# A two-layer decode step on one core: wo in longer runs, o permuted by matmuls, a later return of stashed V, rstd moved behind the projections

## The chip, the core and the metric

One core of a Trainium2 chip runs the whole program. The metric is the device time of one execution in microseconds (us): 214.02 us, the median of three runs (213.67 to 215.77). The engines: TensorE (PE; its weight loads are shown apart as PEld), VectorE (DVE), ScalarE (ACT), GpSimd (POOL), and SyncE (SP), which here only issues DMAs.

## What is computed

Four sequences decode one token each (B = 4, D = 512) through four residual steps: attention, GLU, attention, GLU. Both attentions use the same weights and the same K and V, and so do both GLUs.

```python
def attention(x, k_cache, v_cache, wq, wo):      # Hq=32, Hkv=8, Dh=128, Sk=8192
    W = 2048                                     # the last 2048 keys
    q = (x @ wq) as [B, Hq, 1, Dh]
    k, v = the last W keys of each of 8 heads, each used by 4 query heads
    p = softmax(q k^T * Dh**-0.5);  o = p v
    return o as [B, 1, Hq*Dh] @ wo

def glu(x, w_gate, w_up, w_down):                # F=1792
    return (sigmoid(x @ w_gate) * (x @ w_up)) @ w_down

x = x + attention(layernorm(x), ...);  x = x + glu(layernorm(x), ...)
x = x + attention(layernorm(x), ...);  x = x + glu(layernorm(x), ...)
```

All inputs are bf16. K and V of the window are 16.8 MB each, wq and wo 4.2 MB each, the three GLU weights 5.5 MB together.

## The kernel before

**Memory.** SBUF holds an arena of 50 slots of 128 partitions x 4 KB. K takes 32 of them for good, four a head (two tiles, each with two batches): it is loaded once, transposed in place by DVE in the first attention (`k_transpose`, L676 to L681), and used by both attentions. The other 18 slots make nine tiles of 1 MB. Through these pass, in the order of the list `loads`: wq (4 tiles), V of the first attention (16 tiles, two a head) with the four tiles of wo between them, the GLU weights (w_gate 2, w_up 2, w_down 2), wq again (4), V of the second attention in reversed order of heads, the GLU weights again. The four wo tiles stay from the first attention to the second, and so does one V tile of head 7 (KEEP_V). The other V tile of head 7 is stashed: at the end of the first attention four DVE transposes (`stash`, L490 to L496) put it into the PSUM banks 0 to 3, and four more (`load_stash`, L498 to L509) bring it back into a tile for the second attention.

**Who decides the order.** The program is written as a list of operations with tokens for what they read and write (`P.op`). When the last use of a tile is written down (`done`, L416), its slot goes to the next entry of `loads` at once (`fill`), so each transfer has one slot and waits for that slot's last readers; SP issues transfers strictly in that order. The other engines' orders come from a planner (`_schedule`, L86), a list scheduler that gives each operation a duration from the table `_TM`, and lets an engine pick, among the operations that could start within 60 ns of the earliest, the one written first. At run time each engine follows its fixed order and waits on semaphores.

**Layer norm** (L572 to L612), with x transposed (features on partitions, 4 column groups x 4 batches): DVE squares x and sums x and x squared over the groups (L577, L581); PE adds over partitions with a matrix of ones (L586); DVE makes mean, mean squared and variance (L589 to L595); ACT takes Ln and Exp (L598, L601) for the reciprocal deviation rstd; DVE subtracts the mean and multiplies by rstd into xn (L604, L609).

**q** (`q_proj`, L616 to L660), in two halves of four KV heads: 16 matmuls with xn as weights and wq as moving data (L628); a DVE transpose (L636) and a scaled copy to qh (L641); 16 small matmuls that repeat each head's q on four groups of 32 partitions (L652); an ACT copy to qrep (L659). For each head, `q_unit` then writes four blocks of 32 x 64 into the block-diagonal qbd, two by DVE (L670) and two by ACT (L673).

**One head of attention** (`softmax_unit`, `turn_p`, `pv_unit`, `wo_unit`): 16 score matmuls (L699) into a PSUM bank; DVE maximum (L707, L710, L713); ACT Exp with sums (L716); four permuting matmuls (L728), an ACT copy (L733) and a DVE transpose (L737) turn the probabilities; POOL splits the sums in three parts (L741 to L745), PE spreads them (L751), DVE takes the reciprocal (L758). Then 2 x 32 matmuls with V tiles as weights (L772), a DVE multiplication by the reciprocal (`oe`, L780) into onb, and 16 matmuls with wo as weights (L796) with 4 moving columns each (one query head's four batches), all heads and query heads summing into 16 columns of one PSUM bank. The scores of head ui+2 are written down ahead of the PV of head ui. After the last head DVE adds the sum to x (L834).

**GLU** (`glu`, L837): 16 matmuls each for w_gate and w_up (L854), a DVE transpose each (L861), the sigmoid as Exp, Ln(1+e), Exp(-) on ACT (L867, L870, L873), the product hT on DVE (L876), and the w_down matmuls, L931 in the first GLU and L907 in the last, after which two copies (L915, L917) and a DMA give the output.

The loads that the change or the prediction speak of:

```python
461  def load_wq(k):      # k == 1: tiles of two 4 KB runs a partition
476  def load_wo(hh):
477      load(("wo", hh), 4, "bw_1k", (2 * SLOT, wo_d[:, hh * 2 * REP:(hh + 1) * 2 * REP, :], False))
...
429  def load_k(h):       # 8 transfers of 256 KB a head
```

## Time and profile before

| | |
|---|---|
| median of three runs | 214.02 us (213.67 to 215.77) |
| profiled execution, by the device's clock | 214.02 us |
| its span, first to last instruction | 212.3 us |
| PE, DVE, ACT, POOL busy | 102.0, 90.2, 35.7, 14.7 us |
| read from HBM | 71.83 MB, 338 GB/s over the span |
| first attention | about 14 to 137 us |
| first GLU | about 137 to 149 us |
| second attention | about 152 to 200 us |
| last GLU and output | about 200 to 212 us |

The profile's page gives the busy share of each engine in 40 slices of 5.3 us, the chain of waits that ended last, and groups of instructions by line, with their idle time and what ended it. A table of stretches gives, for any stretch in us from the start: its length, the busy time of PE, PEld, DVE, ACT and POOL with the number of instructions, then the clock granted to TensorE, the DMA share and GB/s. A line of the timeline gives start, duration, engine, line, operation, what it writes and reads, shape and count, and in brackets the idle time before it with its releaser. A line of the waits gives who waited for whom, then total us, times and the longest. The trace also holds each DMA packet with size and duration.

### The profile page before, as it was taken

What the parts mean: (1) busy time and instruction counts of PE and PEld (TensorE: products, weight loads), DVE (VectorE), ACT (ScalarE), POOL (GpSimd) and SP (SyncE); (2) the same over time, 40 slices, a digit from 0 to 9 for tenths busy, and PEclk for the clock granted to TensorE, in tenths of its full rate; (3) what the DMA queues carried; (4) which work ended last, traced back from release to release, by engine and by line L of the source; (5) the groups of instructions that cost most, each with busy time, mean ns of one, the idle gap of its engine ahead of it and who ended that gap; (6) DMA issues with size and microseconds to landing.
All of it is one profiled execution on the core that took longest, in us unless ns stands there. A gap on an engine that the chain in (4) does not pass through costs nothing.

```text
span 212.3 us, 4510 instructions
## 1 busy us (share of the span) xinstructions
PE 102.0 (48%) x1944; PEld 56.3 (27%) x1944; DVE 90.2 (42%) x221; ACT 35.7 (17%) x100; POOL 14.7 (7%) x77
## 2 busy tenths in 40 slices
PE   0440304082450630540620455554368899996675
PEld 0000001041230220230220234412112455665622
DVE  5135778336448217328214430521367443541230
ACT  2002012131030300020110020020024443322020
POOL 4000001101010100010100010000001211111000
PEclk9999999999999999999999999999997555555555
DMA  6999999999999999999999999969999999999990
GB/s 225 420 346 279 279 281 288 411 292 306 350 319 348 350 318 338 258 266 396 283 276 308 348 423 403 377 218 389 360 417 414 412 425 421 418 415 409 406 372 27
DMA packets 16148, 72.13 MB, mean 340 GB/s; under 512 B 1912, under 2 KB 6016, under 8 KB 9472
## 3 DMA queue, kind: packets, MB, share of 16 engines
q1 hardware_dynamic: 16120, 71.84, 96.5%
q8 instruction: 15, 0.25, 0.5%
q14 instruction: 5, 0.04, 0.1%
q10 hardware_dynamic: 8, 0.00, 0.0%
HBM read 71.83 MB, written 0.00 MB: 338 GB/s over the span
## 4 chain that ended last, share of the span: by engine, by line
SPq 44%; DMA 33%; PE 17%; issue 3%; DVE 2%; ACT 1%
SPq L382 44%; DMA arena<-in_A_v_cache_dram 16%; DMA arena<-in_B_w_down_dram 12%; PE ps L699 5%; PE ps L772 5%; DMA arena<-in_A_wq_dram 5%; PE ps L728 2%; PE ps L907 1%; PE ps L796 1%; PE ps L628 1%; PE ps L931 0%; PE ps L854 0%; PE ps L751 0%; ACT prow L716 0%; DVE ebuf L636 0%
## 5 line engine op out<-in xcount | busy, mean ns | idle before, releaser
L772 PE MATMUL ps<-ebuf,arena 128*128 128x8 bf16 x1024 | 31.6, 168 | 52.2 <-DMA arena<-in_A_v_cache_dram 49.2
L680 DVE STREAM_TRANSPOSE arena<-arena 128x1024 f32<-128x1024 f32 x32 | 38.3, 1225 | 19.1 <-DMA arena<-in_A_k_cache_dram 19.1
L772 PEld LDWEIGHTS ps<-ebuf,arena 128*128 128x128 bf16 x1024 | 29.4, 104 | 59.1 <-DMA arena<-in_A_v_cache_dram 55.5
L699 PE MATMUL ps<-arena,qbd 128*16 128x512 bf16 x256 | 29.3, 602 | 25.7 <-DVE qbd L670 13.0
L707 DVE TENSOR_REDUCE nmax<-ps 128x1 f32<-128x512 f32 x16 | 11.0, 687 | 25.5 <-PE ps L699 25.5
L716 ACT ACTIVATE prow<-ps,nmax 128x512 bf16<-128x512 f32 x16 | 11.0, 687 | 48.6 <-DVE nmax L713 26.8
L699 PEld LDWEIGHTS ps<-arena,qbd 128*16 128x16 bf16 x256 | 6.4, 107 | 39.0 <-issue 24.9
L780 DVE TENSOR_TENSOR onb<-ps,rinv 128x16 bf16<-128x16 f32 x16 | 3.1, 192 | 31.9 <-PE ps L772 31.9
L673 ACT COPY qbd<-qrep 32x64 bf16<-32x64 bf16 x32 | 7.7, 241 | 52.7 <-PE ps L699 52.1
L741 POOL CAST s<-psm 128x1 bf16<-128x1 f32 x16 | 3.0, 186 | 172.3 <-ACT prow L716 172.3
L628 PE MATMUL ps<-arena,xn 128*4 128x512 bf16 x64 | 8.2, 610 | 8.0 <-DMA arena<-in_A_wq_dram 6.5
L733 ACT CAST prow<-ps 128x512 bf16<-128x512 f32 x16 | 9.4, 585 | 14.3 <-PE ps L728 14.2
L796 PE MATMUL ps<-onb,arena 128*128 128x4 bf16 x256 | 9.2, 167 | 2.4 <-DVE onb L780 2.4
L737 DVE STREAM_TRANSPOSE ebuf<-prow 128x256 f32<-128x256 f32 x16 | 6.8, 427 | 7.4 <-ACT prow L733 7.3
L728 PE MATMUL ps<-prow,perm 64*128 64x256 bf16 x64 | 9.3, 389 | 1.4 <-ACT prow L716 1.4
L796 PEld LDWEIGHTS ps<-onb,arena 128*128 128x128 bf16 x256 | 8.1, 104 | 3.3 <-DVE onb L780 2.0
L854 PE MATMUL ps<-arena,xn 128*4 128x448 bf16 x64 | 6.6, 564 | 4.7 <-DVE xn L609 3.1
L598 ACT ACTIVATE lnv<-lnv 128x4 f32<-128x4 f32 x4 | 0.8, 206 | 33.0 <-DVE lnv L595 33.0
L636 DVE STREAM_TRANSPOSE ebuf<-ps 128x512 f32<-128x512 f32 x4 | 2.9, 716 | 8.0 <-PE ps L628 7.8
L861 DVE STREAM_TRANSPOSE ebuf<-ps 128x448 f32<-128x448 f32 x4 | 2.6, 650 | 7.8 <-PE ps L854 6.9
L670 DVE COPY qbd<-qrep 32x64 bf16<-32x64 bf16 x32 | 5.3, 165 | 0.7 <-ACT qrep L659 0.2
L751 PEld LDWEIGHTS ps<-sel_b,s 128*128 128x128 bf16 x48 | 2.5, 106 | 8.2 <-issue 5.9
(61 smaller groups left out, 71.0 us busy)
## 6 DMA issues: line engine op xcount, KB each, us to landing
arena<-in_A_v_cache_dram SPq DMA_DIRECT2D x30, 1024.0 KB, 18.3
arena<-in_A_k_cache_dram SPq DMA_DIRECT2D x64, 256.0 KB, 16.8
arena<-in_A_wq_dram SPq DMA_DIRECT2D x8, 1024.0 KB, 9.6
arena<-in_A_wo_dram SPq DMA_DIRECT2D x4, 1024.0 KB, 25.2
arena<-in_B_w_gate_dram SPq DMA_DIRECT2D x4, 896.0 KB, 19.2
arena<-in_B_w_up_dram SPq DMA_DIRECT2D x4, 896.0 KB, 15.8
arena<-in_B_w_down_dram SPq DMA_DIRECT2D x2, 1024.0 KB, 12.4
arena<-in_B_w_down_dram SPq DMA_DIRECT2D x1, 768.0 KB, 6.8
```

The lines of the kernel that those rows point to most:

```text
L382: o = P.op("sync", name, 0.0, lambda e, dst=dst, src=src: e.dma_start(dst, src), r=r, w=w, dma_bytes=nbytes, dma_rate=tm[rate])
L628: last = pe.matmul(ps[32 * hh:32 * hh + NB, qb, :], xn[:, c * NB:(c + 1) * NB], tile_ap(s)[:, o + hh * 512:o + (hh + 1) * 512], start=(c = ...
L673: P.op("scalar", "qe%s_%d" % (tag, a), c_act(64), lambda s_, dst=dst, src=src: s_.copy(dst, src), r=rd, w=[("q", k2, a)])
L680: P.op("vector", "T%d_%d" % (h, t), c_dve(1024), lambda v, v32=v32: v.transpose(v32, v32), r=[("k", 4 * h + t // 2 * 2, x) for x in range( ...
L699: last = pe.matmul(ps[32 * gi:32 * gi + NR, bank, :], qbd[:, q0:q0 + NR], kt[:, cp // 2, cp % 2, b % 2], start=(cp == 0), stop=(cp == 3))
L707: lambda v: v.tensor_reduce(nmax[:, k2:k2 + 1], ps[:, bank, :], AXX, ALU.max),
L716: lambda a: a.activation(prow[:, :].rearrange("p (m x t) -> p m x t", x=16, t=2), ps[:, bank, :].rearrange("p (m t x) -> p m x t", x=16, t ...
L728: last = pe.matmul(ps[:, PBS[i], 0:256], perm[64 * i:64 * i + 64, jh * 128:(jh + 1) * 128], prow[64 * i:64 * i + 64, jh * 256:(jh + 1) * 2 ...
L733: lambda a: a.copy(prow[:, :].rearrange("p (y i t) -> p i y t", i=2, t=2), ps[:, PBS[0]:PBS[0] + 2, 0:256].rearrange("p i (y t) -> p i y t ...
L737: lambda v: v.transpose(ebuf[:, k2 * 256:(k2 + 1) * 256], prow[:, :].bitcast(F32)),
L772: last = pe.matmul(ps[:, ob, bp * 8:bp * 8 + 8], src[:, j * 128:(j + 1) * 128], ev[:, j % 2, j % 16 // 2, x0:x0 + 8], start=(j == 0), stop ...
L796: last = pe.matmul(ps[:, WB, c * NB:(c + 1) * NB], tile_ap(s)[:, o + r_ * D + c * 128:o + r_ * D + (c + 1) * 128], ov[:, r_ * NB:(r_ + 1) ...
```

## The change

- **wo.** A partition now holds four neighbouring rows of wo for a head, so that a run in HBM is 4 KB (REP = 4 rows of 1 KB) where it was 1 KB. Row 4p+m of a head's 512 lies on partition p, so o is to be brought into the same order: four matmuls with 0/1 matrices `permo` (`pm`) copy rows of o, a DVE multiplication with the mask `maskp` (`oq`) keeps the right query head in each 32-partition group, and the result onp has 16 columns for each m. The wo matmuls move 16 columns for 4, into 64 PSUM columns; after the last head a DVE reduction (`xr`) sums the four query heads, ahead of the addition to x.
- **Layer norm.** xn is x minus the mean, from PSUM directly; rstd is left out of it. The variance is computed afterwards from the centred squares (`ln_sq`, `ln_rd2`), summed by PE (`ln_var`) after the first group of projection matmuls, and ACT makes rstd with the score scale folded in. rstd multiplies q in the copy to qh, and the gate's argument (`gs`); in the GLU the up branch gets it through the denominator: 1 / ((1 + e) * std), by `ga` and a DVE reciprocal `gr`, which stand for two ACT functions.
- **q.** The 16 repeating matmuls, qrep and the four block copies a head go. For each head four matmuls (`qx`) with shifted identity weights of 32 rows write the block-diagonal form into one PSUM bank, and one ACT copy of 256 columns moves it to qbd.
- **Stash.** The stashed V tile comes back two loads later in the list, after two V loads in place of ahead of them; its four transposes, in another order of banks, also wait for the first qc of the second attention. The first scores of the second attention go to a bank of q (OBS[0], partly cleared by `zero_q`), not to bank 0, which holds the stash.
- Set-up: `eyew`, `maskp`, `permo` are made from the identity, which now lies in ebuf; eg lies in qbd; a constant 1/D replaces the ones in the norm's sums.

No line of `load_k` or `k_transpose` is in the diff.

```diff
-    wo_d = A_wo.rearrange("(q p) n -> p q n", p=128)
+    wo_d = A_wo.rearrange("(h p m) n -> p h (m n)", p=128, m=REP)
...
-            load(("wo", hh), 4, "bw_1k", (2 * SLOT, wo_d[:, hh * 2 * REP:(hh + 1) * 2 * REP, :], False))
+            load(("wo", hh), 4, "bw_4k", (2 * SLOT, wo_d[:, hh * 2:(hh + 1) * 2, :], False))
...
-                for n, b in enumerate(STASH):
+                for n, b in [(n, STASH[n]) for n in (1, 2, 3, 0)]:
...
-                    o.prio += 60
-                    if n == 3:
-                        after_q.append(o)
+                    o.deps.update(fresh)
...
+            P.op("tensor", "ln_sum" + tag, tm["pe_f32"],
+                 lambda t: t.matmul(mean, ones_d, lnr[:, 0:nb], start=True, stop=True),
...
+            P.op("vector", "ln_xn" + tag, ds,
+                 lambda v: v.tensor_tensor(bview(xn[:, :], b0, b1), bview(xT[:, 0:NX], b0, b1),
+                                           mean.unsqueeze(1).broadcast_to([128, NC, nb]), ALU.subtract),
...
+            def variance():
+                P.op("tensor", "ln_var" + tag, tm["pe_f32"],
+                     lambda t: t.matmul(msq, ones_d, lnr[:, NB:NB + nb], start=True, stop=True),
...
+                P.op("scalar", "ln_ln" + tag, c_act(NB),
+                     lambda a: a.activation(lnv[:, 0:nb], msq, ACTF.Ln, bias=EPS * sc, scale=sc),
+                P.op("scalar", "ln_rstd" + tag, c_act(NB),
+                     lambda a: a.activation(lnr[:, 0:nb], lnv[:, 0:nb], ACTF.Exp, scale=-0.5),
+                if not for_q:
+                    P.op("scalar", "ln_std" + tag, c_act(NB),
+                         lambda a: a.activation(lnd[:, 0:nb], lnv[:, 0:nb], ACTF.Exp, scale=0.5),
...
+                if variance is not None:
+                    variance()
...
+                     lambda v, qi=qi: v.tensor_tensor(
+                         qi.rearrange("p (b x) -> p b x", b=NB),
+                         ebuf[:, :].rearrange("p (x y) -> p y x", y=32)[:, 0:NB],
+                         lnr[:, 0:NB].unsqueeze(2).broadcast_to([128, NB, 4 * REP]), ALU.mult),
...
+                if k and n == 0:
+                    fresh.append(qc)
+                    P.op("vector", "zero_q", c_dve(160), lambda v, qb=qb: v.memset(ps[:, qb, 0:160], 0.0), r=[("qh", i)], w=[("pss", 2)], banks=(qb,))
+                    after = (qc,)
...
-            for a in range(4):
-                dst = qbd[32 * a:32 * a + 32, k2 * 256:(k2 + 1) * 256].rearrange(
...
+            def e_qx(pe):
+                for a in range(4):
+                    last = pe.matmul(dst[:, :, :, a * REP:(a + 1) * REP], eyew[32 * hh:32 * hh + 32, 96 - 32 * a:224 - 32 * a],
+                                     src, start=True, stop=True)
+            P.op("tensor", "qx" + tag, 250.0, e_qx, r=[("qh", h // 4), ("eyew",)], w=[("cb",)], banks=(CB,))
+            P.op("scalar", "qe" + tag, c_act(256),
+                 lambda a: a.copy(qbd[:, k2 * 256:(k2 + 1) * 256], ps[:, CB, 0:256]),
+                 r=[("cb",)], w=[("q", k2)], banks=(CB,))
...
+            bank, pt = (OBS[0], 2) if u == HKV else (SB[k2], k2)
...
+            def e_pm(pe):
+                for m in range(REP):
+                    last = pe.matmul(ps[:, ob, 144 + m * NR:144 + (m + 1) * NR], permo[:, m * 128:(m + 1) * 128], ov,
+                                     start=True, stop=True)
+            P.op("vector", "oq" + tag, tm["dve_fix"] + 60.0,
+                 lambda v: v.tensor_tensor(
...
-                        last = pe.matmul(ps[:, WB, c * NB:(c + 1) * NB],
+                        last = pe.matmul(ps[:, WB, c * NR:(c + 1) * NR],
-                                         ov[:, r_ * NB:(r_ + 1) * NB], start=(first and r_ == 0 and c == 0),
+                                         ov[:, r_ * NR:(r_ + 1) * NR], start=(first and r_ == 0 and c == 0),
...
+            P.op("vector", "xr%d" % L, c_dve(REP * NX),
...
+                if n == 0:
+                    variance()
...
+                    P.op("vector", "gs%d" % k, c_dve(NH),
+                    P.op("vector", "ga%d" % k, c_dve(NH),
+                    P.op("vector", "gr%d" % k, c_dve(NH) + 60.0,
...
-        load_stash(("V",) + keep[0] + (1,))
...
+                    n_v += 1
+                    if n_v == 2:
+                        load_stash(("V",) + keep[0] + (1,))
```

## The prediction, made before the changed kernel was run

> **What bounds the kernel now.** I read the page's slices first, then a table of stretches, the waits of the DMA queue, and the timeline of TensorE and of the last microseconds.
>
> ```profile
> span 212.3 us, 4510 instructions
> ...
> DMA  6999999999999999999999999969999999999990
> GB/s 225 420 346 279 279 281 288 411 292 306 350 319 348 350 318 338 258 266 396 283 276 308 348 423 403 377 218 389 360 417 414 412 425 421 418 415 409 406 372 27
> DMA packets 16148, 72.13 MB, mean 340 GB/s; under 512 B 1912, under 2 KB 6016, under 8 KB 9472
> ```
>
> The DMA engines are busy in every slice but three: the first, the last, and slice 26 (138 to 143 us). So the time is what the packets take, plus three holes. Busy is not fast: 270 to 350 GB/s in the first 118 us, 415 to 425 at the end.
>
> ```profile
> 20.00:30.00 10.00, 1.89 (x16) 0.44 (x16) 7.02 (x10) 0.48 (x2) 0.00 (x0) 1.00 1.01 278
> 35.00:37.00 2.00, 0.00 (x0) 0.00 (x0) 1.62 (x3) 0.00 (x0) 0.00 (x0) 1.00 1.10 321
> 63.00:66.00 3.00, 0.07 (x3) 0.00 (x0) 2.82 (x4) 0.52 (x1) 0.00 (x0) 1.00 1.09 266
> 92.00:96.00 4.00, 1.76 (x41) 1.16 (x37) 1.61 (x3) 0.58 (x1) 0.29 (x2) 1.00 1.09 271
> 116.00:118.00 2.00, 0.00 (x0) 0.00 (x0) 0.55 (x1) 0.00 (x0) 0.00 (x0) 1.00 1.04 344
> 139.00:142.00 3.00, 2.02 (x24) 0.51 (x24) 0.80 (x2) 0.27 (x2) 0.00 (x0) 1.00 0.38 125
> 151.00:155.00 4.00, 1.40 (x12) 0.21 (x16) 2.00 (x4) 0.39 (x2) 0.00 (x0) 1.00 1.03 422
> 160.00:195.00 35.00, 32.17 (x711) 19.00 (x700) 16.54 (x60) 14.06 (x37) 6.36 (x33) 0.54 1.01 417
> ```
>
> The last two columns are DMA share and GB/s. Row 1 is K alone. Rows 2 to 5 are the four wo tiles, 1 KB runs. Row 7 is wq of the second layer: 128 partitions, two 4 KB runs each. Row 6 is the hole. In row 8 PE is busy 32.2 of 35 us while the stream stays full.
>
> ```profile
> SPq L382 <- PE ps L854: 8.6, 4, 5.5
> ...
> 183.11 1.91 PE L699 MATMUL ps<-arena,qbd 128*16 128x512 bf16 x16
> 184.95 0.25 PE L751 MATMUL ps<-sel_b,s 128*128 128x16 bf16 x3
> 185.05 0.57 PE L796 MATMUL ps<-onb,arena 128*128 128x4 bf16 x16
> 185.47 1.85 PE L772 MATMUL ps<-ebuf,arena 128*128 128x8 bf16 x64
> 187.25 0.61 PE L728 MATMUL ps<-prow,perm 64*128 64x256 bf16 x4
> ...
> 206.74 0.22 DVE L876 TENSOR_TENSOR hT<-ebuf,eg 128x56 bf16<-128x56 f32 x1
> 207.40 2.25 PEld L907 LDWEIGHTS ps<-arena,hT 128*4 128x4 bf16 x28 [1.19 <-DMA arena<-in_B_w_down_dram]
> ```
>
> The hole: wd takes the slot of w_gate, so SP waits (up to 5.5 us) for the first GLU matmuls L854, behind PV, wo and the layer norm. One head of the second attention fills PE without a break, 4.7 us from one L728 to the next. At the end hT is done at 206.96 and PE starts at 207.40, when the last weights have landed: computation is only 0.4 us ahead of the stream. That decides what a shorter stream is worth. The sum is against this execution, 214.02 us by its clock (212.3 span and 1.7 around it), which is the median too.
>
> **The change, part by part.**
>
> *wo.* Same 4.19 MB, but 1,024 packets of 4 KB for 4,096 of 1 KB. In the trace's packet records a 1 KB packet takes 58 ns on average: 4,100 x 58 / 16 engines = 14.9 us, 281 GB/s. At row 7's 422 GB/s, the same tile shape, it is 9.9, a gain of 5.0. But wo was slow (266, 271) in two tiles and less so (321, 344) in two; if a cause beside it slows half of it by 266/344 still, the new time is 5.0 + 6.4 = 11.4, a gain of 3.5. If the cause were all in what lies beside it, the gain is 0. I take 4.2, near row 7 for its shape. The DMA page of the Trainium skill ("DMA: Bandwidth & Descriptors", Specifications) puts the smallest run for line rate at 512 B, by which 1 KB runs lose nothing. The trace has 281 against 422; by the rule the sum would be 4.2 us worse. No stall hides this term: the share is 1.0 in all these rows. Fewer packets can only let SP issue sooner.
>
> *The hole.* From the last PV's end (136.07) to L854 (139.66) is 3.6 us. Added: pm 0.30 (L751's three matmuls took 0.25), oq 0.27 (L641, same 128x64, 0.22 and a hop), xr 0.25 (reduction L581, 0.21). Gone: the square (0.21) and everything between the sum and xn, mean, two small DVE steps, Ln and Exp (1.04). Net -0.4; bounds -0.8 (pm costs nothing) and 0. The second norm (149 to 152) waits for wq landing: no gain. Variance, rstd and the gate's DVE steps lie beside the wait for w_up there (143.84): nothing; without that wait they cost what the end pays below. The first norm and the new masks lie before wq landing (7.0 to 13.4): nothing.
>
> So the stream would end 4.6 us sooner. The second attention starts as wq lands, so the computation moves by the same 4.6, and then:
>
> *PE per head.* qx: four matmuls of 64 columns. L699 moves 512 columns in 0.455 us (16 in 1.82, four at a time), so 0.057 each, 0.23 together; bounds 0.11 (PV's 28 ns each) and 0.40 (L652's whole group alone). pm: 4 at L751's 33 ns, 0.13; bounds 0.11, 0.25. wo with 16 columns for 4: L796 with 4 has 26 ns, L772 with 8 28 ns: nothing; at L751's 33 it is 0.11. Together 0.36 (0.22 to 0.76) in each of some six heads with PE full: +2.2 (1.3 to 4.6). Its cover in the first attention is the wait for V (L772 idle 52 us): nothing there. L728 works in a 64-row mode and its four took 0.54 in that chain, whatever the switch costs there. "TensorEngine Tiling (Array Packing)" of the skill (Tiling Modes, Key Properties) says that a change of tiling mode drains the engine, and qx brings a 32-row mode into each head; with two drains of 0.1 a head (an estimate from the 128 cycles of drain in "TensorE: Matmul & The Clock Gate", Part 2) the sum would be 1.2 worse.
>
> *Start of the second attention.* The four transposes of the stash (L504, 0.70 each) ran at 153 to 157, mostly while DVE waited. Now they need qc and the third wq tile, so they run from 158. DVE had 1.7 free before the first maximum at 160.08; 1.1 stay, ahead of that maximum, its exp and all P turns. Against it: half of the qe copies leave DVE (0.16 each), the 16 replication matmuls (0.30) leave PE twice, the first score matmuls no longer wait for them. But qc now waits for ln_var and two ACT steps, 0.35. Net +0.4 (-0.5 to +1.4). V goes out two loads sooner, but the stream is full there: nothing.
>
> *ACT and DVE per head.* Two copies of 0.24 on ACT become one of 0.37 (L659); two of 0.17 on DVE become oq, 0.22. ACT is under half busy: nothing, if the order holds (a rival).
>
> *End.* The chain PV to L854 is 0.4 shorter. After w_gate PE does ln_var (0.5, L586) ahead of w_up, and gs, ga, gr join DVE ahead of the second transpose: +0.5 (0 to 0.6), now with no landing to hide it.
>
> Computation: 2.2 + 0.4 - 0.4 + 0.5 = +2.7. The slack takes 0.4, so 2.3 is given back. Sum: -4.2 - 0.4 + 2.3 = -2.3, **211.7 us**: the stream no longer ends last, PE does.
>
> K's loads and transposes, named in the change's title, are not in the diff: the 64 issues of 256 KB and 278 GB/s stay.
>
> **Rivals.**
>
> *The additions hide.* If qx and pm fall into PE's gaps (1.7 us of "issue" at 194, 0.45 at 177), the stream's 4.6 all show: 214.0 - 4.6 = 209.4. For: those gaps. Against: the 4.7 us chain without a break.
>
> *wo does not get faster.* If something beside it sets its pace, as K's 8 KB packets crawl at 278, only the hole is won: 214.0 - 0.4 + 2.3 = 215.9. For: rows 3 and 4 against 2 and 5. Against: row 7, and all four wo rows lie below it.
>
> *PE waits in its own queue (the other side).* qx, the copy on ACT and the scores now form a chain. If the planned order puts the scores next behind qx, PE waits for ACT: up to an exp (0.88) and a copy (0.37), less 0.35 of overlap, 0.9 a head. Six heads: +5.4, 217.1. Behind it stand PV and wo, whose slots SP wants. It decides from 0.4 a head (2.3 / 6). For: one bank holds qx, and PE is in order. Against: qx of a head needs only the copy of the head before, so it can go a whole head early.
>
> **How the numbers follow.** Given back in part, 0.57 (own range 210.0 to 213.5); additions hidden 0.18; wo no faster 0.14; PE waits 0.11. About 1%, 2.1 us, is what a measurement of this kernel can tell from no change. Faster by that (under 211.9): 0.30 of the first and 0.18: 0.48. Slower (over 216.2): 0.11 and 0.02 of the third: 0.13. Within: 0.39. For 8 in 10 the range takes the hidden case down to 209.0 and the third up to 216.0.
>
> **What would show it.** Right: wo stretches over 380 GB/s and no 1 KB packets; SP not blocked behind wo; the hole about 0.4 shorter; wq landing 4 to 5 us sooner; 5.0 to 5.1 us from L728 to L728 in the second attention; at the end L907 released by DVE, not by DMA. Wrong: wo stretches still under 300; PE idle before the scores with ACT's copy as releaser; L907 still waiting for wd; the first exp of the second attention over 1.5 us later behind the stash.

## The result and the profile after

The changed kernel takes 225.56 us (224.46 to 228.06, four runs) against 213.84 us (212.83 to 215.77, four runs) for the kernel before, measured beside it: 1.052 times as long, 95% interval 1.042 to 1.062. The prediction was 211.7 us, faster, with a range to 216.0. It is wrong in sign. The profiled execution took 225.87 us. Times are medians of all runs of a kernel, ratios compare only the executions within 1.5% of each kernel's fastest, and a row marked * in the table of the experiments has its trace from an execution slower than that.

The page of the changed kernel, cut to its DMA lines:

```profile
span 224.1 us, 4627 instructions
...
DMA  6999999999999999999999977869999999999940
GB/s 238 427 319 281 278 275 360 369 276 370 262 314 388 262 291 304 244 324 318 273 274 355 382 270 276 287 228 376 362 429 366 415 418 424 420 415 402 412 195 1
DMA packets 13076, 72.13 MB, mean 322 GB/s; under 512 B 1912, under 2 KB 1920, under 8 KB 6400
```

The 1 KB packets are gone (under 2 KB: 6016 before, 1920 now), as the edit says. But where the kernel before had one slice below 9 between the ends, there are four in a row (7, 7, 8, 6, from 129 to 151 us), and there the rate falls to 228 to 287 GB/s. The same stretch in the table of stretches, columns as before the prediction (the last two are DMA share and GB/s); first the changed kernel, with wo's four tiles ahead of it and a stretch of K alone behind it, then the kernel before:

```profile
36.00:38.00 2.00, 0.00 (x0) 0.00 (x0) 2.00 (x3) 0.00 (x0) 0.00 (x0) 1.00 1.06 420
64.00:67.00 3.00, 0.48 (x18) 0.39 (x15) 1.91 (x4) 0.50 (x1) 0.00 (x0) 1.00 1.01 318
95.00:98.00 3.00, 0.90 (x32) 0.76 (x29) 1.14 (x3) 1.15 (x3) 0.57 (x3) 1.00 1.04 280
120.00:122.00 2.00, 0.42 (x16) 0.33 (x13) 0.26 (x1) 0.00 (x0) 0.00 (x0) 1.00 0.99 352
...
127.00:151.00 24.00, 14.75 (x303) 9.85 (x303) 9.30 (x27) 2.09 (x7) 0.76 (x4) 1.00 0.77 271
20.00:30.00 10.00, 2.28 (x20) 0.64 (x20) 6.83 (x8) 0.37 (x1) 0.00 (x0) 1.00 1.01 276
```

```profile
127.00:151.00 24.00, 11.72 (x252) 8.01 (x252) 6.75 (x24) 1.18 (x6) 0.00 (x0) 1.00 0.89 342
```

The first wo tile is as fast as forecast (420), the next two are not, and from 127 to 151 us the DMA engines stand still for almost a quarter of the time. The landings say when the time was lost: the second layer's last wq tile lands at 159.7 us before and at 168.1 after, +8.5; the last weights at 209.2 and 217.7, again +8.5. So 8.5 us are gone by the end of the first attention and its GLU, and none in the second attention's stream. The output is issued 11.75 us later, so 3.3 more come after the last landing.

**Where the stream loses it.** The trace keeps 16 completion times for each of these transfers; I read them as one for each of the 16 DMA engines. They show what the page's mean over 16 engines hides. Each row is one transfer of the changed kernel, its 16 completions sorted, in us:

```
wo0   38.1 38.1 38.1 38.1 38.2 38.2 38.2 38.2 38.2 38.2 38.2 38.3 38.3 38.3 38.4 39.8
V     40.6 40.6 40.6 40.6 40.6 40.7 40.7 40.7 40.7 40.7 40.7 40.7 40.8 40.8 40.8 42.3
V     43.1 43.1 43.1 43.2 43.2 43.2 43.2 43.3 43.3 43.3 43.4 43.4 43.4 43.5 43.5 46.8
K     44.1 44.1 44.2 44.2 44.3 44.3 44.4 44.4 44.4 44.4 44.4 44.4 44.5 44.5 44.7 47.5
```

One engine alone is late: 1.4 us at wo0, 3.3 after two V tiles. The fifteen moved their share of the second V tile in 2.5 us (40.6 to 43.1), the late one took 4.5 (42.3 to 46.8). While it was at it, the fifteen were already in K, whose 256 KB transfers land 0.95 us apart (the row from 20 to 30 us above: 276 GB/s). Behind each V pair the distance grows; I call first to last completion the spread. After the 2nd, 4th, 6th and 8th V tile it is 3.7, 5.5, 8.0 and 11.0 us, and 15.5 at its largest. The other engines do not stay together either: at the eighth V tile the three next to last are over 3 us behind the first, and the last 11. When the late engine has no K beside it, it keeps pace: from 131 to 141 us it needs 2.5 us for each tile, and in the second attention, where V follows V, the spread stays at 2.9 us.

A tile is used, and its slot reused, only at its last completion: two V tiles have theirs at 114.4 and 128.6 us, where PE starts on them after waiting.

```profile
114.40 1.02 PE L783 MATMUL ps<-ebuf,arena 128*128 128x8 bf16 x32 [5.06 <-DMA arena<-in_A_v_cache_dram]
128.62 1.01 PE L783 MATMUL ps<-ebuf,arena 128*128 128x8 bf16 x32 [8.20 <-DMA arena<-in_A_v_cache_dram]
```

SP in turn waits for these matmuls (L783) before it can send the next tile into the slot; its waits from 119 to 140 us:

```profile
SPq L385 <- PE ps L783: 18.9, 4, 10.3
```

So from about 128 us most engines have nothing to do, since the slots wait for the last one: those are the holes. The kernel before has the same thing in a milder form: 3.5, 4.1, 4.9, 6.8, largest 8.7.

### The profile page after: what moved, and what is told of

It is laid out like the page before. It is cut to its first block, busy times and chain, and to the rows that moved or that the text cites. A ratio compares the mean times of both kernels' runs of the same rounds, so it can differ in the third digit from the quotient of the medians.

```text
span 224.1 us, 4627 instructions
## 1 busy us (share of the span) xinstructions
PE 109.7 (49%) x2016; PEld 63.3 (28%) x2016; DVE 91.6 (41%) x209; ACT 31.2 (14%) x78; POOL 15.3 (7%) x79
## 2 busy tenths in 40 slices
DMA packets 13076, 72.13 MB, mean 322 GB/s; under 512 B 1912, under 2 KB 1920, under 8 KB 6400
## 4 chain that ended last, share of the span: by engine, by line
DMA 44%; SPq 23%; PE 23%; DVE 5%; issue 4%; ACT 1%; DVEq 0%; ACTq 0%
DMA arena<-in_A_v_cache_dram 27%; SPq L385 23%; DMA arena<-in_A_k_cache_dram 8%; PE ps L783 7%; PE ps L710 6%; DMA arena<-in_A_wq_dram 4%; DMA arena<-in_B_w_up_dram 4%; PE ps L884 2%; PE ps L739 2%; PE ps L822 2%; PE ps L643 1%; DVE ps L496 1%; DVE arena L691 1%; PE ps L942 1%; PE ps L679 1%
## 5 line engine op out<-in xcount | busy, mean ns | idle before, releaser
L783 PE MATMUL ps<-ebuf,arena 128*128 128x8 bf16 x1024 | 32.5, 168 | 49.5 <-DMA arena<-in_A_v_cache_dram 46.2
L783 PEld LDWEIGHTS ps<-ebuf,arena 128*128 128x128 bf16 x1024 | 29.8, 104 | 56.7 <-DMA arena<-in_A_v_cache_dram 52.8
L710 PE MATMUL ps<-arena,qbd 128*16 128x512 bf16 x256 | 28.7, 593 | 30.6 <-DVE arena L691 30.1
L710 PEld LDWEIGHTS ps<-arena,qbd 128*16 128x16 bf16 x256 | 6.4, 108 | 42.2 <-DVE arena L691 30.7
L791 DVE TENSOR_TENSOR onb<-ps,rinv 128x16 bf16<-128x16 f32 x16 | 3.0, 187 | 36.3 <-PE ps L783 36.3
L684 ACT CAST qbd<-ps 128x256 bf16<-128x256 f32 x16 | 5.9, 372 | 54.4 <-PE ps L710 48.1
L822 PE MATMUL ps<-onp,arena 128*128 128x16 bf16 x256 | 9.4, 174 | 1.5 <-DVE onp L806 1.0
L739 PE MATMUL ps<-prow,perm 64*128 64x256 bf16 x64 | 9.3, 388 | 0.7 <-ACT prow L727 0.7
L822 PEld LDWEIGHTS ps<-onp,arena 128*128 128x128 bf16 x256 | 8.1, 104 | 4.8 <-issue 3.1
L654 DVE STREAM_TRANSPOSE ebuf<-ps 128x512 f32<-128x512 f32 x4 | 2.9, 717 | 13.4 <-PE ps L643 13.3
L620 ACT ACTIVATE lnv<-ps 128x4 f32<-128x4 f32 x4 | 0.7, 174 | 51.5 <-PE ps L616 51.5
L679 PE MATMUL ps<-qh,eyew 32*128 32x64 bf16 x64 | 5.9, 224 | 2.8 <-ACT qbd L684 1.4
L806 DVE TENSOR_TENSOR onp<-ps,maskp 128x64 bf16<-128x64 f32 x16 | 3.5, 220 | 6.2 <-PE ps L801 6.1
L762 PE MATMUL ps<-sel_b,s 128*128 128x16 bf16 x48 | 3.7, 175 | 4.5 <-DVE onp L806 4.1
## 6 DMA issues: line engine op xcount, KB each, us to landing
arena<-in_B_w_up_dram SPq DMA_DIRECT2D x4, 896.0 KB, 15.8
arena<-in_B_w_down_dram SPq DMA_DIRECT2D x2, 1024.0 KB, 12.7
```

What stands on the lines that cost most here:

```text
L679: last = pe.matmul(dst[:, :, :, a * REP:(a + 1) * REP], eyew[32 * hh:32 * hh + 32, 96 - 32 * a:224 - 32 * a], src, start=True, stop=True)
L710: last = pe.matmul(ps[32 * gi:32 * gi + NR, bank, :], qbd[:, q0:q0 + NR], kt[:, cp // 2, cp % 2, b % 2], start=(cp == 0), stop=(cp == 3))
L739: last = pe.matmul(ps[:, PBS[i], 0:256], perm[64 * i:64 * i + 64, jh * 128:(jh + 1) * 128], prow[64 * i:64 * i + 64, jh * 256:(jh + 1) * 2 ...
L783: last = pe.matmul(ps[:, ob, bp * 8:bp * 8 + 8], src[:, j * 128:(j + 1) * 128], ev[:, j % 2, j % 16 // 2, x0:x0 + 8], start=(j == 0), stop ...
L822: last = pe.matmul(ps[:, WB, c * NR:(c + 1) * NR], tile_ap(s)[:, o + r_ * D + c * 128:o + r_ * D + (c + 1) * 128], ov[:, r_ * NR:(r_ + 1) ...
```

## The experiments

Two sorts of small packets come into the stream beside the tiles: the page's queue q8 (16 KB, about 1.1 us, fetches of TensorE's instructions; one about every 256 instructions of PE, a matmul and its weight load being two) and q14 (8 KB, 0.3 to 0.5 us). That q8 is TensorE's is read from the runs that put more matmuls at the head of PE's queue: its first packet moves from 36.1 us to 28.6 (e13) and 20.7 (e7). I take q14's first packet to be DVE's, since e10's 15 memsets on DVE move it from 54.2 to 38.3; its second to fourth keep their place in the program there, so they may be another engine's, and the order of e2 and e6 moves the first one too (41.2, 39.9).

The table holds all runs. "PE" is when the first three 16 KB packets come, "DVE" the first 8 KB one after the start, "spread" that after V tiles 2, 4, 6, 8 and the largest, "wq" the last landing of the second layer's wq. The last four columns are of one execution each, and rows of two runs say little alone: the kernel before, measured beside e9 to e12, ranged from 208.4 to 224.9 us in nineteen runs, five of them over 220.

| run | median us (range; runs) | before, measured beside it | PE | DVE | spread | wq |
|---|---|---|---|---|---|---|
| before | 213.84 (212.8-215.8; 4) | | 36.2 53.3 76.7 | 40.1 | 3.5 4.1 4.9 6.8, 8.7 | 159.7 |
| after | 225.56 (224.5-228.1; 4) | 213.84 | 36.1 56.1 77.5 | 54.2 | 3.7 5.5 8.0 11.0, 15.5 | 168.1 |
| e1 | 211.59 (211.0-214.7; 8) | 212.9 | 36.3 53.9 78.7 | 40.3 | 3.5 3.7 3.6 3.7, 3.7 | 156.9 |
| e2 | 214.13 (213.5-214.8; 2) | 212.9 | 36.7 55.2 74.9 | 41.2 | 3.7 3.9 3.5 3.8, 3.9 | 157.1 |
| e3 * | 222.2 (219.9-224.5; 2) | 212.9 | 36.8 56.4 77.9 | 55.0 | 3.6 4.9 6.3 9.7, 11.4 | 167.4 |
| e4 * | 213.57 (211.9-215.3; 2) | 212.9 | 37.0 54.6 80.6 | 41.2 | 3.7 4.0 3.9 4.1, 4.1 | 160.4 |
| e5 | 227.74 (225.7-229.8; 2) | 216.13 | 36.0 55.8 76.7 | 54.3 | 3.7 5.3 7.5 10.8, 14.4 | 167.2 |
| e6 * | 213.82 (211.5-216.2; 2) | 216.13 | 35.7 53.1 73.7 | 39.9 | 4.0 4.8 5.0 6.1, 8.2 | 159.5 |
| e7 | 211.44 (210.0-212.9; 2) | 216.13 | 20.7 49.7 63.4 | 52.3 | 2.8 3.6 3.4 4.2, 4.8 | 153.6 |
| e8 * | 224.49 (222.8-226.2; 2) | 216.13 | 35.4 55.4 76.4 | 53.9 | 4.0 6.1 7.8 10.7, 13.4 | 168.4 |
| e9 * | 224.75 (216.3-233.2; 2) | 214.36 | 6.7 38.2 59.3 | 57.0 | 5.6 6.7 9.8 12.8, 15.8 | 176.0 |
| e10 * | 219.34 (216.5-222.2; 2) | 214.36 | 37.4 57.5 77.5 | 38.3 | 4.0 4.5 4.8 6.4, 8.2 | 163.1 |
| e11 * | 212.4 (207.9-218.3; 8) | 214.36 | 19.0 50.8 67.7 | 42.9 | 3.1 3.6 3.8 4.1, 4.3 | 160.1 |
| e12 * | 212.14 (206.4-217.3; 10) | 214.36 | 21.2 53.4 67.9 | 55.7 | 3.5 4.5 4.2 4.9, 5.2 | 160.3 |
| e13 | 211.79 (211.4-212.2; 2) | 215.59 | 28.6 52.1 66.9 | 54.2 | 2.5 3.0 3.5 3.5, 3.5 | 155.8 |
| e14 | 235.49 (234.2-236.8; 2) | 215.59 | 6.9 46.9 65.1 | 55.3 | 5.5 7.9 11.7 13.9, 17.0 | 173.3 |
| e15 * | 222.1 (218.9-225.3; 2) | 215.59 | 21.1 53.4 68.1 | 55.9 | 3.4 4.8 5.5 7.4, 10.2 | 164.7 |
| e16 | 216.78 (213.2-220.3; 2) | 215.59 | 20.4 49.9 63.8 | 52.3 | 3.1 4.1 4.0 4.3, 4.3 | 153.0 |
| e17 | 212.3 (209.4-223.5; 12) | 213.6 | 28.6 54.4 65.5 | 53.4 | 3.3 3.9 3.8 4.2, 5.3 | 154.3 |
| e18 * | 212.37 (202.9-213.3; 6) | 213.6 | 29.6 53.3 67.2 | 42.2 | 2.3 3.2 3.2 3.3, 3.3 | 157.4 |

**Is it wo's run length?** Theory S: wo's 4 KB runs alone take the engines out of step. Rival C: it is the rest of the change. e1 is the kernel before with only wo's two lines in the new form (wo's rows then do not match o's); e2 the changed kernel with only these two lines in the old form (the same holds); e3 and e4 are the changed kernel and the one before with a limit on how far SP runs ahead.

```diff
-    wo_d = A_wo.rearrange("(q p) n -> p q n", p=128)
+    wo_d = A_wo.rearrange("(h p m) n -> p h (m n)", p=128, m=REP)
...
-            load(("wo", hh), 4, "bw_1k", (2 * SLOT, wo_d[:, hh * 2 * REP:(hh + 1) * 2 * REP, :], False))
+            load(("wo", hh), 4, "bw_4k", (2 * SLOT, wo_d[:, hh * 2:(hh + 1) * 2, :], False))
```

> The kernel before with only wo loaded in 4 KB runs (rows of wo then lie in another order than o, so the output is not the reference's; all instructions and sizes are those of before). The changed kernel lost 8.5 us by the landing of the second layer's wq (168.1 against 159.7 us) and 3.3 more after it. Theory S (step of the 16 DMA engines): with 1 KB runs SP stood still behind each wo tile for 11 to 18 us and the engines stayed within 8.7 us of each other; with 4 KB runs it runs ahead, the engines part by up to 15.5 us, a V tile is whole only when the last engine is done, and slots come free late. Then this kernel alone shows the loss: wq lands at 166 to 169, total 219 to 223 us. Rival C (the longer chain of computation in the first attention, qx, copy, pm, frees V tiles later): the loss stays away, total 208 to 213 us.

> The changed kernel with wo loaded in 1 KB runs as before (rows of wo and o then do not match, so the output is not the reference's). Theory S: the 8.5 us come back, spread under 9 us, wq lands at 159 to 161, and only the 3.3 us of the second attention and last GLU are left: 216 to 218 us. Rival C: nothing comes back, 224 to 227 us.

```diff
+            ahead, sent = (), 0
+            for q in sent_dma[::-1]:
+                if sent >= 3145728:
+                    ahead = (q,)
+                    break
+                sent += q.dma_bytes
...
-                     r=r, w=w, dma_bytes=nbytes, dma_rate=tm[rate])
+                     r=r, w=w, dma_bytes=nbytes, dma_rate=tm[rate], after=ahead)
```

> The changed kernel, where SP also waits, ahead of each transfer, for the last landing of the transfer that lies 3 MB back, so that no engine can run further ahead than that. Theory S: the spread stays under about 9 us, the holes at 127 to 150 us go, and the first attention ends as before or sooner, total 213 to 219 us. Rival L (the 4 KB layout of wo itself makes some engines slow, by its addresses): SP's waits only add holes, 224 us or more.

> The kernel before with the same limit of 3 MB. Theory S: the spread, up to 8.7 us there, shrinks too; the first attention ends up to 3 us sooner, 210 to 214 us. If a limit only costs (waits that leave DMA engines idle): 215 us or more.

e1 is no slower than the kernel before: ratio 0.997 (0.990 to 1.003), spread 3.7. Theory S as stated has fallen. But C has fallen too, since e2, with all the rest of the change, is 214.1, ratio 1.011 (0.998 to 1.024). Each half alone is harmless, both together cost 8.5 us. The limit of 3 MB didn't hold the engines together in the changed kernel (spread 11.4), so e3 tells little of what a tighter one would do; that wasn't tried. In the kernel before the spread was 4.1 under the limit, for 8.7 without (e4), and the time, 213.6 for 212.9, no shorter.

**The order, and the packets.** What a wo tile does besides: `load_wo` gives the planner a rate ("bw_4k" for "bw_1k"), and from it comes a slightly different fixed order of instructions. Between e2 and the changed kernel one DVE operation (oq against a K transpose) and one PE group (qx against a PV block) stand the other way round. The rate altered e1's order too: a block of PV matmuls and two small DVE operations stand elsewhere than in the kernel before. e6 and e8 cross the two: 4 KB runs in e2's order, and 1 KB runs (wo's rows then do not match o's) in the changed kernel's order. e5 is the changed kernel again. e7 leaves the order as it is and puts 54 small matmuls at the head of PE's queue, into unused columns, before x has come; it moves only the count at which instruction packets come.

```diff
-            load(("wo", hh), 4, "bw_4k", (2 * SLOT, wo_d[:, hh * 2:(hh + 1) * 2, :], False))
+            load(("wo", hh), 4, "bw_1k", (2 * SLOT, wo_d[:, hh * 2:(hh + 1) * 2, :], False))
```

(e6; e8 is e2 with "bw_4k" in that place.)

```diff
+            def e_pad(t):
+                last = None
+                for _ in range(54):
+                    last = t.matmul(ps[:, CB, 448:452], ident, ident[:, 0:4], start=True, stop=True)
+                return last
+            P.op("tensor", "pad", 0.0, e_pad, r=[("e", 0)], w=[("cb",)], banks=(CB,))
```

> The changed kernel, unaltered, once more, beside the three kernels of the same call. Every theory that puts the loss into the program expects 224 to 228 us and a spread between a transfer's first and last completion that grows past 10 us during the first attention. If the 8.5 us belonged to the chip or to the hour, it would come at 213 to 216.

> The changed kernel with wo in 4 KB runs, but with the planner told the rate of 1 KB runs for wo, so that the instructions stand on every engine in exactly the order of the run with wo in 1 KB runs (214.1 us). Theory O (the order that the planner picked from the higher rate is the seed: one K transpose and one q spread stand elsewhere): 213 to 216, spread stays under 5 us. Theory R (the 4 KB runs themselves are needed for the loss): 222 to 228, spread past 10 us.

> The changed kernel with 54 small matmuls more at the head of PE's queue, before x is there, so that the 16 KB packets that fetch PE's instructions come some 8 us earlier (near 28 and 48 us in place of 36 and 56 us). Theory F (an instruction packet that falls into the V transfers of an engine that is already behind makes it fall further behind): the spread no longer grows at the V pair that lands near 57 us and the time leaves 224 to 228 by 3 us or more, most likely to 214 to 219. If the packets do not matter: 224 to 228 and the same growth at the same transfer.

> The counterpart: wo in 1 KB runs (rows of wo that do not match those of o, so the output is not the reference's), with the planner told the rate of 4 KB runs, so that the instructions stand in the changed kernel's order. Theory O: 222 to 228, spread past 10 us. Theory R: 213 to 216, spread under 5 us.

e5 repeats the loss. e6 and e8 settle the cross: the order carries the loss, 213.8 in e2's order with 4 KB runs, 224.5 in the changed kernel's order with 1 KB runs. All ten runs with the changed kernel's order (after, e3, e5, e8) took 219.9 us or more, all four with e2's (e2, e6) 216.2 or less. Theory R (the 4 KB runs are needed) has fallen. Theory O holds but for its size: e6's spread grew to 8.2, not under 5. And e7, with the same order as the changed kernel but for the padding, comes at 211.4, 14 to 16 us below it. The traces show no other difference at the start: every engine's operations stand in the same order behind the padding, and the first matmul with wq starts at 5.9 us, for 5.6 and 5.7 in the two profiles of the changed kernel. So it isn't the order as such; what the padding moves is the instruction packets.

**Is it the phase?** 128 matmuls are 256 instructions, one whole period of PE's packets; e10 is meant to move DVE's packet alone; e11 pads the kernel before; e12 is e7 with more rounds.

```diff
-                for _ in range(54):
+                for _ in range(128):
```

```diff
+        for _ in range(15):
+            P.op("vector", "padv", 0.0, lambda v: v.memset(perm[:, 0:4], 0.0), w=[("perm",)])
         P.op("vector", "zero_perm", 100.0, lambda v: v.memset(perm[:], 0.0), w=[("perm",)])
```

> The changed kernel with 128 small matmuls at the head of PE's queue, in place of the 54 that gave 211.4 us. A matmul counts as two instructions (a load of weights and the matmul), and a 16 KB packet comes about every 256 instructions of PE, so 128 matmuls put the packets back where the changed kernel has them, near 36 and 56 us. Theory F (the time of PE's instruction packets against the V transfers decides): 222 to 228, spread past 10 us. Rival W (any work on PE ahead of the start, or a warmer PE, is what helped): 209 to 214, as with 54.

> The changed kernel with 15 small memsets more on DVE during set-up, so that the 8 KB packet that fetches DVE's instructions comes some 15 instructions earlier: near 41 us as in the kernel before, in place of 54 us, 2 us ahead of PE's. PE's packets stay near 36 and 56 us. If both packets together between 54 and 56 us are the seed: 211 to 217, spread under 8 us. If PE's packet at 56 us is enough: 222 to 228 and spread past 10 us.

> The kernel before with the same 54 matmuls at the head of PE's queue. Its own profile shows the spread growing to 8.7 us. Theory F: the time of the kernel before is itself a draw from the same mechanism; with the packets moved the spread stays under 6 us and the time is 208 to 213, at or below the fastest runs of the kernel before. If the packets matter only to the changed kernel: 213 to 216.

> The changed kernel with 54 matmuls at the head of PE's queue (211.4 us in two runs), with more rounds, to see whether it beats both kernels. Theory F: 209 to 214, ratio to the kernel before 0.98 to 1.00. If the two runs were luck of the draw, some of its runs come at 216 or more.

Rival W (work ahead of the start helps) has fallen, with e14 below: more of the same work brings the loss back, here in one of e9's two runs (233.2 us, spread 15.8; the other took 216.3). But not only for the reason I gave: there is a packet at 6.7 us that I hadn't counted, and the engine is late from then on. e10 answers in between, 219.3 and spread 8.2, and neither of my two expectations was met. That fits DVE's packet being part of it, but PE's came 1.3 us later too (37.4 and 57.5), and the memsets change the order of DVE's set-up, so e10 doesn't part the two. e11 is 0.982 (0.974 to 0.991) of the kernel before, by two of its runs against three, and 212.4 for 214.4 in the medians: a hint that the kernel before itself carries some of this loss, no more. e12 keeps a spread of 5.2, but with 0.988 (0.964 to 1.011) it isn't shown to beat the kernel before.

**Two more doses, and the end.** e13 and e14 have 27 and 96 matmuls. e15 and e16 are e7 with qx, or pm, done twice in the second attention alone.

```diff
-                for a in range(4):
+                for a in list(range(4)) * (2 if tag[0] == "2" else 1):
...
-                for m in range(REP):
+                for m in list(range(REP)) * (2 if tag[0] == "2" else 1):
```

(The first pair of lines is e15, the second e16.)

> The changed kernel with 27 small matmuls at the head of PE's queue. Theory F: PE's first two packets come near 29 and 50 us, both while K streams (K lands from 16 to 36 and from 44 to 54 us), so the spread stays under 7 us and the time is 208 to 215. If the dose of 54 was luck: anything, 216 to 228 as likely as not.

> The changed kernel with 96 small matmuls. Theory F: PE's packets come near 12, 40 and 61 us, the second while V lands and no engine is yet behind, the third while K streams; none falls into the V pair that lands near 57 us, so the spread stays under 8 us and the time is 209 to 217. If only the dose of 54 helps, or any dose past some number hurts as 128 did: 220 to 232.

> The changed kernel with 54 matmuls at the head, and in the second attention alone each q spread done twice (8 matmuls for 4, same result). The time from the last wd landing to the issue of the output was 3.4 to 4.0 us with 54 matmuls alone. If the spread is on the path that sets the end, as the prediction's 0.23 us per head had it: 4.8 to 6.2 us. If it hides in PE's waits: under 4.3 us.

> The changed kernel with 54 matmuls at the head, and in the second attention alone each permutation of o done twice (8 matmuls for 4, same result). If it is on the path, as the prediction's 0.13 us per head had it: 4.2 to 5.5 us from the last wd landing to the issue of the output. If it hides: under 4.2 us.

e13 came as theory F said, e14 didn't: 235.5 for 209 to 217. Its first packet came at 6.9 us, not near 12. Its first matmul with wq starts at 5.8 us, as in e7 (5.9) and e13 (5.6), so the padding doesn't delay the start. The completions show what a packet does. e14's second wq tile, the first to land after the packet at 6.9 us; then e13's K transfers on both sides of the packet at 28.6:

```
wq (e14)   7.9  7.9  8.0  8.0  8.0  8.0  8.1  8.1  8.2  8.2  8.2  8.2  8.2  8.2  8.3  9.7
K  (e13)  28.3 28.4 28.4 28.4 28.4 28.5 28.5 28.6 28.7 28.7 28.7 28.7 28.7 28.7 28.8 28.8
K  (e13)  29.3 29.3 29.4 29.4 29.4 29.5 29.6 29.6 29.7 29.7 29.7 29.7 29.7 29.7 29.8 30.9
```

A packet makes one engine late by about its own length, 1.1 to 1.4 us, and what follows decides. In e13 the late engine has K before and behind it, and the spread at wo0 is 1.2 us (1.8 in the changed kernel). In e14 it is still in wq when the others reach K, and its 1.4 become 3.2 with the fourth wq tile. The page of e13 has no holes:

```profile
span 209.7 us, 4680 instructions
...
DMA  6999999999999999999999999999999999999970
GB/s 226 428 338 267 275 270 262 413 324 277 378 261 307 412 255 294 333 272 344 359 266 324 420 418 411 402 411 409 363 431 392 427 419 416 419 415 406 411 309 1
```

The stretch that stood at 271 GB/s in the changed kernel, in e13:

```profile
127.00:151.00 24.00, 12.93 (x225) 7.38 (x221) 7.94 (x27) 0.72 (x4) 0.00 (x0) 1.00 1.02 400
```

And the DMA answer for the changed kernel from 50 to 60 us, where both packets fall into one V pair:

```profile
q8 instruction: 1, 0.02, 0.8%
q14 instruction: 1, 0.01, 0.2%
```

There the last engine needs 5.2 us for its share of the second V tile (56.5 to 61.7); in e1, whose packets come at 53.9 and 40.3, 4.3 (56.2 to 60.5).

e15 and e16: from the last weights' landing to the output's issue 7.2 us in both, against 3.4 and 4.0 in e7 and e12. That is above both ranges (4.8 to 6.2, and 4.2 to 5.5), and it doesn't show what the added matmuls cost, since e14, with nothing done twice, has 8.3. What differs most is the time that PE stands still with no releaser but "issue", from the second attention's second exp to hT: 5.8 us in e16, 4.3 in e15 and 5.4 in e14, for 2.4 in e7 and 2.8 in e12. The longest in e16 begins at 196.0 us, with a 16 KB packet of PE at 196.4:

```profile
198.86 0.22 PE L789 MATMUL ps<-ebuf,arena 128*128 128x8 bf16 x2 [2.82 <-issue]
```

Where nothing breaks in, pm done twice costs nothing: two heads of e16 take 4.89 and 4.88 us from exp to exp, as in e7, because the 0.11 us more for eight matmuls than for four is gone again in the PV block behind them (0.85 us for 0.97). qx done twice takes 0.53 us from its start to the next group's (189.94 to 190.47 in e15), where one takes 0.32.

**What the change is worth in step.** The changed kernel and the one before, both with 27 matmuls at the head of PE's queue.

> The changed kernel with 27 matmuls at the head of PE's queue (211.8 us in two runs), in five rounds. Theory F: spread under 7 us, 208 to 214 us, ratio to the kernel before 0.975 to 1.0; from the last landing of the second layer's wq to the output's issue 52 to 54 us. If the pad's effect does not hold from run to run: several runs over 220.

> The kernel before with the same 27 matmuls. If the change is worth the 2.3 us of the prediction once both kernels keep in step: 2 us slower than the changed kernel with 27 matmuls in the same call. If wo's longer runs give under 1 us and the computation gives back 2 to 3, as the runs so far say: 0 to 2 us faster than it; from the last landing of wq to the output's issue 50 to 52 us.

212.3 against 212.4 us: no difference that can be told, and e17 is 1.003 (0.996 to 1.010) of the kernel before. One of e18's six runs took 202.9 us, 9 us below the other five; no trace of it is kept, and why isn't known. In the profiles e17's wq lands 3.1 us before e18's, but K, which neither edit touches, ran faster in that execution: 0.906 us a transfer against 0.960, 3.5 us over 64. One of e17's twelve runs took 223.5 us, so the padding doesn't rule the loss out. No version is shown to beat both kernels.

## Why the prediction was wrong

**The step that failed** is in *wo*: "No stall hides this term: the share is 1.0 in all these rows. Fewer packets can only let SP issue sooner", and with it "So the stream would end 4.6 us sooner". It took 16 DMA engines for one, since the page gives their mean. A share of 1.0 in a row doesn't say that all sixteen work on the same transfer. Whether they do depended on fetches of instructions, for which the sum had no term: by the padding alone, which moves them, the same kernel took 212 or 235 us. The stream ended 8.5 us later, none of it through longer packets of wo: e8, with 1 KB runs, lost as much.

**The size of wo.** In step, with a spread that stays under 5.5 us, the term is small. I took the mean completion of each wo tile less that of the transfer ahead of it, summed over four: 12.7, 12.8 and 12.6 us with 1 KB runs (e2, e11, e18), 11.3, 11.3, 11.5 and 11.7 with 4 KB (e1, e13, e7, e17). So a gain of about 1.3 us, below the 4.2 and inside its 0 to 5.0. The 14.9 us that I started from was a sum of packet durations; in e2, in step, the packets still sum to 14.7 us while the four tiles take 12.7. Packets overlap in an engine, as the shares of 1.09 and 1.10 in wo's rows of the kernel before could have told. And the new tile doesn't reach row 7's pace: 11.3 for 9.9. By the Trainium skill's 512 B as the smallest transfer for line rate ("DMA: Bandwidth & Descriptors", Specifications) the gain would be 0; that was off by 1.3 us here, my row by 2.9.

**The hole**: the chain came out as forecast, -0.4, but it wasn't what made the hole. From the last PV's end to the gate's first matmul it took 3.6 us before, and 3.2 (144.50 to 147.66) now:

```profile
143.49 1.01 PE L783 MATMUL ps<-ebuf,arena 128*128 128x8 bf16 x32 [1.46 <-DMA arena<-in_A_v_cache_dram]
144.79 0.28 PE L801 MATMUL ps<-onb,permo 128*128 128x16 bf16 x4 [0.29 <-DVE onb L791]
145.39 0.59 PE L822 MATMUL ps<-onp,arena 128*128 128x16 bf16 x16 [0.32 <-DVE onp L806]
146.72 0.59 PE L597 MATMUL ps<-lnr,inv_d 128*128 128x4 f32 x2 [0.74 <-DVE lnr L594]
147.66 1.66 PE L884 MATMUL ps<-arena,xn 128*4 128x448 bf16 x16 [0.36 <-DVE xT L604]
```

In e1, whose computation is that of the kernel before and whose engines stay in step, SP waits for L854 just as long (up to 5.5 us), and there is no hole:

```profile
135.00:140.00 5.00, 2.96 (x26) 0.81 (x26) 1.35 (x6) 1.14 (x5) 0.00 (x0) 1.00 1.04 390
140.00:145.00 5.00, 1.93 (x40) 1.03 (x40) 0.87 (x2) 0.02 (x1) 0.00 (x0) 1.00 1.00 412
```

e11 and e18 show the same. So by these traces the hole of the kernel before came from the late engine too, and a shorter chain gains the stream nothing in step.

**What is given back** was near in sum and wrong in its parts, so that the sum agrees is luck. From wq's last landing to the output's issue the kernel before takes 51.1 us (50.5 to 51.5 in before, e1, e11, e18), the changed kernel 53.4 (52.2 to 54.2 in after, e2, e7, e12, e13, e17): +2.3, the number of the prediction. The other profiles of its computation have 53.3 to 55.6, and e14 57.5; with them and e4 the difference is 2.9. Its stages, as means over the runs first named:

| stage | before | after | measured | predicted |
|---|---|---|---|---|
| wq landing to first exp | 2.4 | 3.9 | +1.5 | +0.4 |
| first to eighth exp | 28.2 | 30.7 | +2.6 | +2.2 |
| eighth exp to hT | 17.2 | 16.0 | -1.2 | +0.1 |
| hT to the output's issue | 3.3 | 2.7 | -0.6 | -0.4 (slack) |

*Start of the second attention*: the stash does come ahead of the first maximum, as the prediction had it, but the q transpose of the other half now stands in DVE's queue ahead of it too. Timeline of DVE in the changed kernel:

```profile
165.53 0.19 DVE L666 MEMSET ps<- 128x160 f32 x1
166.94 2.51 DVE L506 STREAM_TRANSPOSE arena<-ps 128x512 f32<-128x512 f32 x4 [1.22 <-PE ps L643]
169.68 0.72 DVE L654 STREAM_TRANSPOSE ebuf<-ps 128x512 f32<-128x512 f32 x1 [0.24 <-PE ps L643]
170.32 0.65 DVE L718 TENSOR_REDUCE nmax<-ps 128x1 f32<-128x512 f32 x1
```

The maximum at 170.32 is 2.2 us behind the landing (168.13); in the kernel before it was 0.4 behind (160.08 after 159.65), and the transpose came after it.

*PE per head*: where nothing breaks in, 4.88 us from exp to exp (the same from L739 to L739, 181.67 to 186.55), near the 5.0 to 5.1 forecast; in the kernel before 4.64, so +0.24 for the 0.36. The first two heads are 0.4 to 0.6 us shorter than before, and one is 7.4 for 4.7 (7.2 from L739 to L739, 192.04 to 199.24), since the order puts three blocks of PV into it where the others have two. Hence the -1.2 of the stage behind: the two stages belong together, +1.4 for the +2.3 forecast. Timeline of PE:

```profile
192.04 0.61 PE L739 MATMUL ps<-prow,perm 64*128 64x256 bf16 x4
192.58 0.39 PE L679 MATMUL ps<-qh,eyew 32*128 32x64 bf16 x4
192.90 0.28 PE L801 MATMUL ps<-onb,permo 128*128 128x16 bf16 x4
...
197.33 0.59 PE L783 MATMUL ps<-ebuf,arena 128*128 128x8 bf16 x16 [0.46 <-issue]
```

The 4.88 us hold one pm and no qx, which the order puts ahead of these heads and into the long one. So a head with pm and the wider wo matmuls costs 0.24 more, for the 0.13 forecast for pm (upper bound 0.25), though e16 shows that it isn't a price for each matmul; qx takes 0.32, from its start to the next group's (192.58 to 192.90), for 0.23. No drain for the tiling mode is needed to explain 4.9 us, so the Trainium skill's rule that a change of mode drains the engine ("TensorEngine Tiling (Array Packing)", Tiling Modes) isn't shown at the 1.2 us worked out from it. The rival *PE waits in its own queue* didn't come about: qx of a head runs well ahead.

*End*: right in the changed kernel, where the last weights (217.7 us) are there before hT. Timeline of the changed kernel:

```profile
219.52 0.22 DVE L911 TENSOR_TENSOR hT<-ebuf,qbd 128x56 bf16<-128x56 f32 x1
...
219.88 1.30 PE L942 MATMUL ps<-arena,hT 128*4 128x256 bf16 x16 [0.63 <-DVE hT L911]
```

In step it isn't so sure: in e17 hT is done at 203.6 us, 1.0 ahead of the last landing, so there the stream still ends last.

So with the engines in step the sum is -1.3 + 2.3 = +1.0, the hole's 0.4 not being won, and e17 against e18 measured -0.1, the same within what these runs can tell. That lies nearer to the prediction's rival *wo does not get faster* (+1.9) than to its sum (-2.3). The 11.7 us of the result are a thing apart: 8.5 from the spread, and 3.3 from the computation that no longer hides behind the stream.

**The signs.** No 1 KB packets: right. wo over 380 GB/s: in one tile of four. SP not blocked behind wo: right (V is issued at 18.9 and 19.5 us, before at 18.9 and 29.8) and worth nothing (e8, blocked, and the changed kernel lost the same). wq 4 to 5 us sooner: wrong.

**What stays open.** That the late engine is slowed in V by the others in K is read from the times (4.5 us for what they did in 2.5, and 2.5 again where no K runs beside it), not tried by a run with a faster K. Which engine fetches instructions, and whether PE's packets always take the same one, the records don't say; that one and the same engine stays last would fit it, but the completions carry no engine's name. The growth isn't a sharp rule of the second packet's time either: e10, with PE's packet at 57.5, lost half of what the changed kernel did, and e2, with 55.2, nothing. Runs with a spread of up to 4 after the fourth V tile stayed under 5.5 (e1, e2, e4, e7, e11, e13, e17, e18), and those with 4.9 or more grew past 11 (after, e3, e5, e8, e9, e14); between lie e6, e10, e12, e15 and e16, and the kernel before at 4.1, which grew to 8.7.

## What to carry to other kernels

A stream that keeps all DMA engines busy is as fast as its last engine: before summing packets, look at the first and last completion of each transfer, and where they drift apart, treat the time as a draw that any edit may change. When a small edit moves the time by far more than its own terms, pad one engine's instruction queue by half a fetch period and by other doses before blaming the edit. And an edit that is meant for the stream must be judged on two landings, the one that ends the stage and the last one, since what it gives the stream the computation can take back.

## What the runs showed of the hardware

- A 16 KB instruction packet takes 0.9 to 1.4 us and leaves one engine late by 1.1 to 1.4 us (28.6 us in e13, 6.9 us in e14).
- One late engine of sixteen moved 64 KB of V in 4.3 to 5.2 us while the others, moving on to K, had needed 2.5.
- 27 or 54 matmuls of 4 columns ahead of the work, under 2 us on an idle engine, moved the changed kernel from 226 to 212 us; 96 moved it to 235. The first matmul with wq started at 5.6 to 5.9 us in all of them.
- In the second attention PE stands still with no releaser but "issue", 2.17 us at 207.85 in the changed kernel, with a 16 KB packet at 207.4, and 2.4 to 5.8 us in all in e7 and e16. I read it as PE waiting for its instructions; no run tried that.
- K's pace differs between executions of unchanged K code: 0.906 us for 256 KB in e7 and e17, 0.97 in e1 and e13, some 4 us over the kernel's 64 transfers.
